# Softmax of the queries for a whole group at once, with a newly searched order

## The chip, the cores and the metric

The kernel runs on one core of one Trainium2 chip. The time is that of one execution on the device, in microseconds (us); the profile is of one further execution on the same core, and its own times run from the first to the last instruction (the span). The engines are TensorE (PE; PEld is its load of weights), VectorE (DVE), ScalarE (ACT), GpSimd (POOL) and SyncE (SP), which here only issues transfers.

## The reference

Two parts follow one another. In the first, q, k and v have 8 batches, 8 heads, 576 positions and 64 features. q is put through a softmax over its 64 features, k through one over the positions; then each head multiplies its k (transposed) with v, and q with that 64x64 result. In the second, the 8 heads side by side make 4608 rows of 512 features, which pass a feed-forward layer.

```python
q_s = np.exp(q - np.max(q, axis=-1, keepdims=True))
q_s = q_s / (np.sum(q_s, axis=-1, keepdims=True) + 1e-09)
k_s = np.exp(k - np.max(k, axis=2, keepdims=True))
k_s = k_s / (np.sum(k_s, axis=2, keepdims=True) + 1e-09)
kv = np.einsum('bhsd,bhse->bhde', k_s, v)
attn = np.einsum('bhsd,bhde->bhse', q_s, kv)
x = attn.transpose(0, 2, 1, 3).reshape(B * S, H * D)
h = x @ w_in                                  # 512 -> 2048
out = (h / (1.0 + np.exp(-1.702 * h))) @ w_out  # 2048 -> 512
```

## The kernel before, in words

The 4608 rows are cut into 12 tiles of 384 (t = 0 to 11), three rows to a partition. A tile's q comes in two groups of four heads (i = 0, 1): 128 partitions with 4 heads x 3 rows x 64 features, 768 values each, in the buffer qt[i]. There are thus 24 groups of q, each with 12 softmaxes to a partition.

`q_stats` makes the softmax of one group. VectorE takes the 12 maxima, with the sign turned, into stat (run_m, L659). ScalarE then executes 12 exponentials of 64 values, each with its own maximum as bias and with a sum taken on the way (run_e, L667: an ACTIVATE and a read of the accumulator each); for the planner these are three or four separate pieces. VectorE adds 1e-9 and takes reciprocals (run_r, L675 and L676). In tiles 0 and 1 VectorE scales the group (run_n, L684) and TensorE transposes it (q_tr, L737). In later tiles (TURNED = 2) a copy of q that is stored turned in DRAM comes in as qT; `spread_out` transposes the statistics (L695), writes them to DRAM (dm and ds, L702), and GpSimd's transfers bring them back spread over partitions (L718): the maxima are added to qT by the transfer itself, then ScalarE takes the exponential of qT (L725, 128x768); the reciprocals overwrite qt, and x_raw (L753) multiplies the product with them.

`k_max` and `k_sub` do the softmax of k (maxima over positions through GpSimd; L552 to L558, L576, L581). `kv_pairs` (L614) multiplies k and v, `x_pairs` (L803) multiplies q with the result.

All matrix products of the feed-forward layer are made from two rounded parts of each operand, a high and a low one, in three matmuls (high-high, high-low, low-high). So every value passes a rounding cast on ScalarE and a subtraction on VectorE (L1265 and L1268, L840 and L843, L1137 and L1140) before TensorE can use it. Weights come in 64-bit form and are converted first (`conv_w`: L439, L443, L447, L454, L464), then stored to DRAM and read back when needed (`refill`, L903). Tiles 0 and 1 run plainly (`g1`, L831; `g2`, L863). From tile 2 on, tiles go in pairs through seven products (`product`, L1230) in place of eight, from sums and differences of the blocks of x (`t_make`, L1083; `x_split`) and of the weights: `s_make` (L1026 to L1041) makes and stores those of w_in, `w_make` (L974 to L1004) those of w_out, once, while tiles 2 and 3 run, from w_out blocks that are refilled for it. For tiles 2 and 3 the second matrix runs plainly (L1494), from tile 4 on in seven products too (`stream` and `still_part`, both through L1366). Results leave through copies (L876, L1456, L1467, L1515) and transfers.

The order of all work is written out by hand. `Plan.add` collects 3333 pieces with engine, cost, buffers read and written, and a function that issues them; the list FIRST gives each piece its place. `Plan.order` walks through the pieces in the sense of this list and issues them, so every engine's queue, and SP's and GpSimd's queues of transfers too, have the order that the list says. A queue executes strictly one after the other: an instruction that waits for a semaphore keeps back all that stand behind it. The costs of `add` serve this walk alone. Rank and table arguments have no further effect on the order once FIRST is given, but ScalarE must load another function table wherever an exponential follows a gelu in its queue, or the other way round.

Of the kernel before, what the change touches and what calls it, by code (L numbers as in the profile page):

```python
# [17 lines left out]
class Plan:  # L18
# [278 lines left out]
def act(n):  # L297
    return 0.19 + n / 1200
# [3 lines left out]
def efficient_attention_then_gelu_ffn(  # L302
# [177 lines left out]
    def bc(a, n):  # L480
        return a.unsqueeze(len(a.shape)).broadcast_to([*a.shape, n])
# [1342 lines left out]
```

## Time and profile before

| | |
|---|---|
| median of 3 runs | 870.77 us (869.83 to 873.27) |
| the profiled execution | 870.66 us |
| its span | 868.9 us, 15873 instructions |
| TensorE busy | 808.8 us (93%) |
| VectorE busy | 564.8 us (65%) |
| ScalarE busy | 581.7 us (67%) |
| GpSimd busy | 166.7 us (19%) |
| mean granted TensorE clock | 0.98 of full speed |
| moved by DMA | 253.72 MB, mean 292 GB/s |
| chain that ended last | TensorE 54%, DMA 21%, VectorE 6%, ScalarE 5% |

A busy time is the union of an engine's instructions, so it counts overlapped ones once. Idle time of an engine matters only if work that the end depends on stands behind it. The names out<-in are the program's tiles: qt, qT and stat are the buffers of the softmax, bank is a PSUM bank, w any weight slot, dwo, dwi, dsl and the like are the copies of weights in DRAM, xc and pu are rounded parts, sl is the scratch of w_make, work and g are temporaries.

### The profile page before, as it was taken

The numbers are of one execution on the slowest core, as the hardware profiler recorded it, in microseconds if no ns is written. First come the engines' busy times: TensorE is split into PE (matmuls) and PEld (weight loads), VectorE is DVE, ScalarE is ACT, GpSimd is POOL, SyncE is SP. The second block draws the span as 40 slices with busy tenths as digits, with TensorE's granted clock in tenths as the row PEclk, the third lists the DMA queues.
The fourth block names the chain that finished last, engine by engine and source line by source line (L and its number), as shares of the span: only waits on it lengthen the run. The fifth ranks groups of instructions, "written<-read, shape, count | busy, mean of one in ns | idle before, by whom it ended". The sixth has DMA issues, their size and how long they took to land.

```text
span 868.9 us, 15873 instructions
## 1 busy us (share of the span) xinstructions
PE 808.8 (93%) x5596; PEld 747.6 (86%) x5596; DVE 564.8 (65%) x1073; ACT 581.7 (67%) x1437; POOL 166.7 (19%) x261
## 2 busy tenths in 40 slices
PE   4799999988899989998999999999999999999998
PEld 3588888767787777787999998999998999999998
DVE  6898953397666577464587755778555497554464
ACT  7988865777675678575687476698576764454443
POOL 1104210534231210232123022222022200000000
PEclk7899999998999999999999999999999999999999
DMA  8998996757999997999988979999789787786861
GB/s 315 409 409 356 330 412 233 186 191 228 372 284 375 297 325 220 343 336 336 319 282 269 322 253 380 297 334 273 240 305 289 251 287 274 234 288 229 300 240 55
DMA packets 98239, 253.72 MB, mean 292 GB/s; under 512 B 14960, under 2 KB 42224, under 8 KB 98160
## 3 DMA queue, kind: packets, MB, share of 16 engines
q1 hardware_dynamic: 86000, 236.72, 75.8%
q0 software_dynamic: 12160, 15.99, 9.5%
q8 instruction: 44, 0.72, 0.3%
q14 instruction: 35, 0.29, 0.1%
HBM read 205.23 MB, written 47.43 MB: 291 GB/s over the span
## 4 chain that ended last, share of the span: by engine, by line
PE 54%; DMA 21%; DVE 6%; ACT 5%; issue 2%; POOL 1%; SPq 1%; DVEq 0%; POOLq 0%; ACTq 0%
PE bank L1230 23%; PE bank L1366 20%; PE bank L1494 4%; DMA qt<-in_q 4%; DMA out<-tmp 3%; DMA qT<-dm 2%; PE bank L831 2%; ACT qt L667 2%; DMA w<-dwo 2%; PE bank L863 2%; DMA w<-dsl 1%; DMA qt<-ds 1%; PE bank L614 1%; DMA w<-dsh 1%; PE bank L803 1%
## 5 line engine op out<-in xcount | busy, mean ns | idle before, releaser
L1230 PE MATMUL bank<-xc,w 128*128 128x384 f32 x1680 | 321.7, 341 | 23.3 <-ACT g L1272 4.8
L1230 PEld LDWEIGHTS bank<-xc,w 128*128 128x128 f32 x1680 | 291.4, 189 | 37.0 <-ACT g L1272 7.6
L1366 PE MATMUL bank<-w,pu 128*128 128x256 f32 x1260 | 163.7, 281 | 1.7 <-DMA w<-dwo 1.2
L1366 PEld LDWEIGHTS bank<-w,pu 128*128 128x128 f32 x1260 | 156.7, 189 | 4.8 <-issue 2.6
L1366 PE MATMUL bank<-w,xc 128*128 128x256 f32 x756 | 102.4, 282 | 4.7 <-DMA w<-dwo 3.3
L1366 PEld LDWEIGHTS bank<-w,xc 128*128 128x128 f32 x756 | 97.0, 189 | 7.7 <-DMA w<-dwo 3.4
L667 ACT ACTIVATE qt<-qt,stat 128x64 f32<-128x64 f32 x288 | 96.4, 337 | 10.2 <-DVE stat L659 7.5
L702 POOL DMA_DIRECT2D dm<-statT x80 | 42.3, 538 | 242.9 <-DVE statT L695 242.6
L831 PE MATMUL bank<-xh,w 128*128 128x384 f32 x256 | 69.5, 341 | 1.3 <-ACT g L837 1.2
L863 PE MATMUL bank<-w,gh 128*128 128x512 f32 x192 | 60.3, 395 | 0.0
L702 POOL DMA_DIRECT2D ds<-statT x80 | 42.8, 607 | 75.1 <-DVE statT L695 74.8
L667 ACT ACTIVATION_READ_ACCUMULATOR qt<-qt,stat 128x1 f32 x288 | 54.4, 189 | 0.0
L718 POOL DMA_DIRECT2D qT<-dm x40 | 38.0, 1075 | 74.0 <-PE bank L1230 37.5
L831 PEld LDWEIGHTS bank<-xh,w 128*128 128x128 f32 x256 | 47.2, 190 | 3.0 <-ACT g L837 2.0
L1272 ACT COPY g<-bank 128x384 f32<-128x384 f32 x52 | 24.8, 477 | 28.3 <-PE bank L1230 22.9
L1272 ACT COPY bank<-bank 128x384 f32<-128x384 f32 x40 | 18.6, 466 | 37.4 <-PE bank L1230 33.4
L831 PE MATMUL bank<-xl,w 128*128 128x384 f32 x128 | 43.3, 338 | 0.0
L863 PEld LDWEIGHTS bank<-w,gh 128*128 128x128 f32 x192 | 35.4, 188 | 8.4 <-issue 1.8
L718 POOL DMA_DIRECT2D qt<-ds x40 | 25.7, 646 | 74.9 <-DMA ds<-statT 20.2
L863 PE MATMUL bank<-w,gl 128*128 128x512 f32 x96 | 38.1, 396 | 1.4 <-DVE gl L843 1.4
L659 DVE TENSOR_REDUCE stat<-qt 128x12 f32<-128x768 f32 x24 | 22.8, 951 | 25.1 <-DMA qt<-in_q 24.9
L1257 ACT ACTIVATE g<-bank 128x384 f32<-128x384 f32 x51 | 25.0, 490 | 21.0 <-PE bank L1230 19.3
(179 smaller groups left out, 1350.0 us busy)
## 6 DMA issues: line engine op xcount, KB each, us to landing
w<-dwo SPq DMA_DIRECT2D x48, 512.0 KB, 5.9
w<-dwb SPq DMA_DIRECT2D x48, 512.0 KB, 5.9
w<-dwi SPq DMA_DIRECT2D x44, 512.0 KB, 6.9
w<-dsl SPq DMA_DIRECT2D x32, 512.0 KB, 6.2
w<-dsh SPq DMA_DIRECT2D x32, 512.0 KB, 6.0
w<-dwa SPq DMA_DIRECT2D x32, 512.0 KB, 6.1
qt<-in_q SPq DMA_DIRECT2D x24, 384.0 KB, 4.8
vt<-in_v SPq DMA_DIRECT2D x14, 650.0 KB, 10.3
```

The source lines that it names most:

```text
L614: nc.tensor.matmul(pk[r0 : r0 + D, m // 2, m % 2], kt[:, o + a, c, :], vt[:, o + a, c, :], start=c == 0, stop=c == CM - 1, tile_position=( ...
L659: nc.vector.tensor_reduce(out=least, in_=qt, axis=AX.X, op=ALU.max, negate=True)
L667: nc.scalar.activation(qt[:, a, b], qt[:, a, b], AF.Exp, bias=least[:, a, b : b + 1], accum_out=sums[:, a, b : b + 1])
L702: nc.gpsimd.dma_start(out=d[:, 32 * b : 32 * b + 32], in_=statT[i][at_ : at_ + M, :])
L718: nc.gpsimd.dma_start(out=out_, in_=src, **more)
L831: nc.tensor.matmul(ph, wi[w][j][:, c, :], x[:, c, :], start=c == 0 and i == 0, stop=c == KC - 1 and i == 2,)
L863: nc.tensor.matmul(po[c], x[:, cs], wo[w][j], start=j == 0 and i == 0, stop=j == NJ - 1 and i == 2)
L1230: nc.tensor.matmul(pb, ws[w][:, c * P : (c + 1) * P], xx[x][:, c * TB : (c + 1) * TB], start=p in FRESH and c == 0 and i == 0, stop=c == 1 ...
L1257: lambda: nc.scalar.activation(d, src, AF.Gelu_apprx_sigmoid), table="gelu")
L1272: plan.add("ACT", act(TB), (PB,), (key,), free_, lambda: nc.scalar.copy(dst, pb))
L1366: nc.tensor.matmul(po, y[:, cs], w, start=start and i == 0, stop=i == 2, skip_group_check=True,)
L1494: nc.tensor.matmul(po[:, f0:f1], x[:, cs], w[:, h * DM + f0 : h * DM + f1], start=m == 0 and e == 0 and i == 0, stop=m == NQ - 1 and e == ...
```

## The change

In `q_stats` the per-head exponentials are taken out of ScalarE's list. VectorE adds the (negative) maxima to the whole group, with the 12 maxima broadcast over 64 features; ScalarE takes one exponential over the group in place; VectorE sums the 12 runs of 64 into stat. The gate, which holds the work back to a stage, moves from the exponentials to the addition. For a group of tiles 2 and up this makes three pieces out of four, for one of tiles 0 and 1 three out of three, so there are 3313 pieces, and FIRST is a new list throughout.

```diff
@@ FIRST: all 3333 places replaced by 3313 others @@
-    1328, 1, 2, 12, 10, 11, 13, 15, 4, 0, 3, 5, 7, 6, 8, 37, 44, 39, 70, 42, 64, 61, 58, 67, 76, 86, 142, 128, 146,
...
@@ in q_stats @@
-        def run_e(a):
-            for b in range(qt.shape[2]):
-                nc.scalar.activation(
-                    qt[:, a, b], qt[:, a, b], AF.Exp, bias=least[:, a, b : b + 1], accum_out=sums[:, a, b : b + 1]
-                )
-
-        for a in range(qt.shape[1]):
-            plan.add("ACT", 0.25 * qt.shape[2], (KM, *gate), (*Q, KS), ranks[1], lambda a=a: run_e(a), table="exp")
+        def run_s():
+            nc.vector.tensor_tensor(out=qt, in0=qt, in1=bc(least, D), op=ALU.add)
+
+        plan.add("DVE", dve(M * D), (KM, *gate), Q, ranks[1], run_s)
+        plan.add("ACT", act(M * D), (), Q, ranks[1], lambda: nc.scalar.activation(qt, qt, AF.Exp), table="exp")
+
+        def run_t():
+            nc.vector.tensor_reduce(out=sums, in_=qt, axis=AX.X, op=ALU.add)
+
+        plan.add("DVE", dve(M * D), Q, (KS,), ranks[2], run_t)
```

How the two lists differ, piece by piece: of TensorE's 730 pieces 443 have another place in its queue, 100 by more than three places and none by more than 16. Of VectorE's pieces that both kernels have, 376 of 1036 move by more than three places, of ScalarE's 169 of 827 (a group's exponentials counted as one), of SP's transfers 174 of 535, of GpSimd's 15 of 137. In the first transfers, the second batch's two k loads are issued before v's instead of behind the weights w_in 0 and w_out 0.

## Rows read from the trace of the kernel before

**Rows 1.** The page: busy us and share by engine; TensorE's costliest group with mean ns.

```profile
PE 808.8 (93%) x5596; PEld 747.6 (86%) x5596; DVE 564.8 (65%) x1073; ACT 581.7 (67%) x1437; POOL 166.7 (19%) x261
...
L1230 PE MATMUL bank<-xc,w 128*128 128x384 f32 x1680 | 321.7, 341 | 23.3 <-ACT g L1272 4.8
```

**Rows 2.** Stretches: us, busy by engine, clock, DMA share, GB/s.

```profile
0.00:34.00 34.00, 18.47 (x175) 13.96 (x176) 24.30 (x48) 26.63 (x102) 5.82 (x9) 0.78 0.91 349
34.00:145.00 111.00, 108.31 (x608) 96.85 (x608) 80.94 (x120) 84.47 (x171) 19.34 (x27) 0.99 0.95 361
145.00:215.00 70.00, 60.76 (x420) 49.99 (x420) 45.57 (x90) 49.74 (x152) 30.57 (x48) 0.93 0.69 202
215.00:375.00 160.00, 146.77 (x809) 125.41 (x808) 107.33 (x220) 111.27 (x284) 34.75 (x57) 0.98 0.94 317
375.00:700.00 325.00, 310.91 (x2385) 298.54 (x2384) 209.06 (x414) 229.12 (x563) 76.17 (x122) 1.00 0.91 298
```

**Rows 3.** TensorE's waits: releaser, us in total, times, longest.

```profile
PE bank L737 <- ACT qt L667: 4.9, 1, 4.9
...
PE bank L1366 <- DMA w<-dwo: 4.5, 2, 3.3
...
PE bank L1230 <- DMA w<-dsl: 2.2, 2, 1.3
```

**Rows 4.** Timeline, TensorE and one of VectorE: start, us, what, [idle before <-releaser].

```profile
158.21 2.55 PE L614 MATMUL bank<-vt,kt 128*64 128x65 f32 x80 [1.27 <-ACT tmp L876]
...
191.10 0.44 PE L1230 MATMUL bank<-xc,w 128*128 128x384 f32 x1 [0.97 <-ACT xc L1137]
...
230.83 0.95 DVE L659 TENSOR_REDUCE stat<-qt 128x12 f32<-128x768 f32 x1 [4.50 <-DMA qt<-in_q]
...
233.88 1.56 PE L803 MATMUL bank<-qT,kvn 64*64 64x192 f32 x16 [3.37 <-issue]
...
263.67 1.64 PE L1230 MATMUL bank<-xc,w 128*128 128x384 f32 x6 [1.96 <-DVE g L1249]
...
306.59 1.31 PE L1230 MATMUL bank<-xc,w 128*128 128x384 f32 x6 [2.94 <-DVE raw L753]
```

**Rows 5.** Groups by line and form: busy us, mean ns, idle before by releaser.

```profile
L659 DVE TENSOR_REDUCE stat<-qt 128x12 f32<-128x768 f32 x24 | 22.8, 951 | 25.1 <-DMA qt<-in_q 24.9
...
L684 DVE TENSOR_TENSOR qt<-qt,stat 128x768 f32<-128x768 f32 x4 | 3.8, 958 | 0.1
...
L725 ACT ACTIVATE qT<-qT 128x768 f32<-128x768 f32 x20 | 16.9, 845 | 4.1 <-DMA qT<-dm 3.2 <-issue 0.8
```

**Rows 6.** VectorE's waits: the first sums of w_make.

```profile
DVE sl L974 <- DMA w<-dwo: 15.8, 11, 4.4
```

**Rows 7.** Groups by line and form, line 667.

```profile
L667 ACT ACTIVATE qt<-qt,stat 128x64 f32<-128x64 f32 x288 | 96.4, 337 | 10.2 <-DVE stat L659 7.5 <-DVE statT L695 2.5
...
L667 ACT ACT_TABLE_LOAD x15 | 19.2, 1283 | 0.7 <-DMA qt<-in_q 0.4
```

**Rows 8.** Line 667 over six stretches of the span: its busy time summed.

```profile
sum 868.90, ACT 120.61; mean ACT 20.10
```

**Rows 9.** Timeline of ScalarE: a table load and the activation behind it.

```profile
182.32 1.28 ACT L725 ACT_TABLE_LOAD   x1
183.61 0.84 ACT L725 ACTIVATE qT<-qT 128x768 f32<-128x768 f32 x1
```

**Rows 10.** Timeline of the start: VectorE, then the first large matmul.

```profile
7.78 0.69 DVE L552 TENSOR_TENSOR tmp<-kt 128x512 f32<-128x512 f32 x1 [2.58 <-DMA kt<-in_k]
...
28.54 1.48 DVE L576 TENSOR_TENSOR ek<-ek,mx 128x1280 f32<-128x1280 f32 x1
...
33.74 0.69 PE L831 MATMUL bank<-xh,w 128*128 128x384 f32 x1
```

**Rows 11.** The page, DMA issues: KB each, median us to landing.

```profile
w<-dwo SPq DMA_DIRECT2D x48, 512.0 KB, 5.9
...
qt<-in_q SPq DMA_DIRECT2D x24, 384.0 KB, 4.8
```

346 rows, old and new, of the table FIRST are left out of this document.

## The prediction, made before the changed kernel was run

> **What bounds the kernel now.** I read the page's busy times first, then a table by stretches, then whom TensorE waited for, then its single idle gaps, each with the queue of the engine that it names. TensorE is busy 808.8 of 868.9 us [rows 1]. The missing 60.1 us is all that a change to VectorE and ScalarE can win, apart from the slow clock in two stretches. The table puts 15.5 us of it into the first 34 us (18.47 busy, granted clock 0.78), 2.7 into the next 111, 9.2 into the turn from 145 to 215 (clock 0.93), 13.2 into 215 to 375 and 14.1 into 375 to 700 [rows 2]; some 5 us lie behind that, where no q is left. No helper is full: ScalarE is busy 67% and VectorE 65%. Both are dense at the start (26.63 and 24.30 of 34).
>
> TensorE's largest single wait is the first transpose of q, 4.9 us; 6.7 us were spent waiting for weights from DRAM, on two rows [rows 3]. The gaps one by one show another cause: at 263.67 and 306.59 TensorE waits 1.96 and 2.94 us for VectorE, and at 233.88 it waits 3.37 us with no releaser named [rows 4]. VectorE itself then stands at the head of its queue waiting for a transfer: the maximum of a q group at 230.83 had waited 4.50 us for the load of q, with other work behind it [rows 4]. Over the run such maxima wait 24.9 us [rows 5], and the first sums of w_make (L974) 15.8 us for w_out blocks [rows 6]. So this is a TensorE-bound kernel whose remaining gaps come from the start, from dense ScalarE and VectorE at the turn, and from transfers that land after the place that the written order gave their reader.
>
> **What is removed and added, in engine time.** Per group of q, 12 activations with a bias and a sum each go. Line 667 holds ScalarE for 120.61 us; without its 15 table loads of 1.283 (19.2) that is 101.4, or 4.22 for each of 24 groups [rows 7, 8]. One exponential of 128x768 takes their place; the same form stands in the trace as L725, 0.845 us. Saved: 24 x (4.22 - 0.85) = 81 us. VectorE gets an addition of 128x768 with a broadcast operand (the form of L684, 0.958) and a sum of 128x768 to 128x12 (the form of the maximum, L659, 0.951) [rows 5]: 24 x 1.91 = 46 us more. From the end of the maximum to the sums it takes 2.8 us instead of 4.2 if nothing stands between.
>
> The searched order also sets how often ScalarE changes its function table: counted in the written order, 58 times before (as many loads as the trace has, 15 of them at L667 [rows 7]) and 64 after; 6 x 1.283 = 7.7 us. ScalarE thus ends near 582 - 81 + 8 = 509 us busy, VectorE near 565 + 46 = 611: the fuller helper is now VectorE.
>
> The trace shows what a switch takes in the queue: a load begins at 182.32, and the activation behind it at 183.61 [rows 9], 1.29 us later. The Trainium skill (ScalarE: Activation LUTs, What ACT_TABLE_LOAD costs) says that about 1.38 us of draining follow each load, 2.66 per switch; by that the six switches would cost 16 us of ScalarE instead of 7.7. The row disagrees, and I go by the row.
>
> **The start (to about 60 us).** Four of the groups lie here. ScalarE gains 4 x 3.37 = 13.5 us, VectorE gets 4 x 1.91 = 7.6 more. On VectorE, the work that leads to the first large matmul (33.74) passes the subtraction for the second batch's k at 28.54 [rows 10]. In the new list five of the new instructions stand ahead of it (4.8 us). The third group's scaling (0.96) and two conversion steps of 128x512 (0.69 each at most, what such a step takes at 7.78) are moved behind it, 2.3. The first addition falls into the 2.58 us in which VectorE waits for k at 7.78 [rows 10], 0.96 covered. Net 4.8 - 2.3 - 1.0 = 1.5 us later; of VectorE's 9.7 us idle in the first 34 [rows 2] some, between 9 and 28 us, can give a part back. The third group's sum and scaling now stand ahead of the transpose that TensorE executes before the second batch's key-value product, and the fourth group's follow among conversions, while TensorE idles only 2.7 of the next 111 us. I take +1.5 in all. The 4.9 us wait for the first transpose hardly shrinks: the first sum stands in VectorE's new list behind three steps for k's maximum, which begin at 7.78, and the next q's maximum; what ScalarE gains is lost there. Bounds: -3 (the loads of the second batch's k are issued ahead of v, and ScalarE stops being a limit, a quarter of its 13.5) to +6.7 (7.6 less the covered 0.96).
>
> **The turn (145 to 215).** Two gaps follow directly on a run of line 667: 1.27 us at 158.21, where a copy of an output bank (L876) stood behind 24 of its activations, and 0.97 at 191.10, where the split of x (L1137) stood behind nine [rows 4]. In the new list the second group's exponential of the third tile stands later, behind such casts. I take both, -2.2. Bounds: 0 to -6, two thirds of the stretch's 9.2 us idle.
>
> **Late transfers.** I counted the steps of TensorE's written order that stand between the issue of a load and its first reader; a step is a product or its like, six matmuls, 6 x 321.7 / 1680 = 1.15 us [rows 1]. Of the 16 refills that w_make reads, 11 had four steps or fewer before, none has after; the median goes from 4 to 9.5. Of the 24 loads of q, those with three or fewer fall from 8 to 5, the median goes from 4 to 5. Of 268 refills that TensorE reads itself, those with four or fewer fall from 11 to 5, and none is left with three. A w_out block lands 5.9 us after its issue, q 4.8 [rows 11]: four steps are too few for the one and about even for the other, nine are enough. So the two gaps behind w_make go (1.96 + 2.94 = 4.9), half of the 3.37 at 233.88 (its load of q has 8 steps instead of 6), and a quarter of the 6.7 us of direct waits, 1.7: together -8.3. Bounds: -15.0 (all of these whole) to +3, one gap of the largest size newly made, since a load issued earlier needs its buffer earlier, and all loads stand in SP's queue behind the one that waits.
>
> **New waits elsewhere.** 20 groups put 38 us on VectorE between 60 and 700 us. Maximum, addition and sum stand in one queue with the splits (L1268) and sums (L1249) that TensorE needs, and the sum waits there for ScalarE's exponential; whatever is behind it is late by that wait. Where the new list leaves a few steps between exponential and sum, as it mostly does, the wait is nothing; I take +1.5, bounds 0 to +5 (a quarter us per group). Of the six table loads I take one on the path, +1.3, bounds 0 to +7.7.
>
> **Sum.** +1.5 - 2.2 - 8.3 + 1.5 + 1.3 = -6.2. The profiled execution took 870.66 us (its span of 868.9 and 1.8 around it), 0.1 below the median of 870.77: 870.77 - 6.2 = 864.6.
>
> **Rivals.**
> - The gaps change places. TensorE executes the same matmuls in nearly the same order (100 of 730 steps move by more than three), and where one wait goes, the next bank may wait for its copy instead. For it: each gap is only 1 to 3 us. Against it: the late transfers are one cause, which the order takes away. Gains of 10.5 shrink to a third, the costs of 4.3 stay: 870.8 - 3.5 + 4.3 = 871.6.
> - Slower: VectorE becomes the limit of the start. Place: its queue from 12 to 60 us, where the conversion of weights waits behind the new instructions. Price: +6.7, with the costs elsewhere (+2.8) against a third of the transfer gain (-2.8): 877.5. It decides when the subtraction for the second batch's k begins after about 31 us and the first large matmul after 37. Against it: conversions of weights needed later can slip at no cost.
> - A large gain: all late-transfer gaps go (-15.0) and the turn gives 3, at the costs of 4.3: 857.1. For it: the shortest distances grow for all kinds of loads. Against it: five refills keep four steps.
>
> **Chances.** Forecast 0.50, places change 0.22, large gain 0.13, slower 0.15. A measurement of this kernel tells about 0.5% from no change, 4.4 us: faster is below 866.4, slower above 875.1. The forecast's own range, 859 to 869, gives 0.46 faster and 0.04 same; the large gain 0.13 faster; the changed places 0.03, 0.16 and 0.03; the slow start 0.01 same and 0.14 slower. Faster 0.62, same 0.21, slower 0.17. The range is 853 to 877: it leaves out about half of the slow case and the ends of the large gain.
>
> **What would show it.** Right: ScalarE near 509 and VectorE near 611 us busy; 64 table loads; VectorE's wait of L974 for w_out down from 15.8 to under 5, and of the maxima for q under 18; no gap of TensorE over 2.5 us between 215 and 375; the first large matmul between 33 and 36.5 us. Wrong: 10 us or more of new gaps in front of VectorE's splits, a first large matmul after 37, or more than 6.7 us of direct waits of TensorE for w_out and low slab refills.

## The result, and the profile after

Before and after were run on one chip: 872.02 us median before (869.83 to 873.81, 4 runs), 840.33 after (838.14 to 845.29, 4 runs). The ratio is 0.9646, with a 95% interval of 0.9595 to 0.9696. The forecast of 864.6 had the direction right and a fifth of the size; the time lies 13 us below the range. The profiled execution of the changed kernel took 840.9 us, its span 839.1. In the table below, ratios leave out runs more than 1.5% above the fastest of their kernel and medians do not, so for f3_old_on_time (870.5 to 888.6 us) the median looks worse than the ratio.

The page first; in the changed kernel most lines behind the softmax stand one number higher.

```profile
PE 800.3 (95%) x5596; PEld 744.8 (89%) x5596; DVE 606.9 (72%) x1121; ACT 515.6 (61%) x891; POOL 166.7 (20%) x261
...
L1231 PE MATMUL bank<-xc,w 128*128 128x384 f32 x1680 | 318.7, 337 | 13.7 <-DVE g L1250 4.2
```

Against [rows 1], TensorE's idle time fell from 60.1 to 38.8 us (839.1 - 800.3), 21.3 of the 29.8 us of span. The other 8.5 us came out of its busy time, with the same 5596 matmuls. VectorE and ScalarE moved as forecast (611 and 509 expected).

The page's groups of the new softmax (line, engine, operation, out<-in, count, busy us, mean ns, idle before):

```profile
L665 DVE TENSOR_TENSOR qt<-qt,stat 128x768 f32<-128x768 f32 x24 | 22.7, 950 | 0.1
...
L668 ACT ACTIVATE qt<-qt 128x768 f32<-128x768 f32 x24 | 20.3, 846 | 6.4 <-DVE qt L665 6.3
...
L671 DVE TENSOR_REDUCE stat<-qt 128x12 f32<-128x768 f32 x24 | 22.7, 947 | 0.9 <-ACT qt L668 0.6
```

The durations taken from the nearest forms [rows 5] were right within 10 ns. The stretches of [rows 2], in the kernel after:

```profile
0.00:34.00 34.00, 18.30 (x177) 14.91 (x178) 28.46 (x53) 16.66 (x28) 4.18 (x8) 0.75 0.95 375
34.00:145.00 111.00, 109.88 (x620) 97.13 (x619) 85.89 (x129) 73.03 (x104) 19.97 (x27) 1.00 0.93 347
145.00:215.00 70.00, 64.50 (x451) 53.84 (x451) 55.18 (x103) 45.87 (x70) 31.30 (x48) 0.95 0.85 253
215.00:375.00 160.00, 155.91 (x963) 136.40 (x962) 127.31 (x248) 107.03 (x183) 41.85 (x66) 1.00 1.00 331
375.00:700.00 325.00, 315.79 (x2404) 306.99 (x2403) 234.96 (x448) 210.60 (x375) 69.40 (x112) 1.00 0.92 306
```

Between 215 and 375 us TensorE executed 963 instructions where it had executed 809. But equal times no longer hold equal work, so I cut both spans where TensorE had done about the same number of instructions (the marks agree within 15). The kernel before:

```profile
0.00:33.74 33.74, 18.21 (x174) 13.70 (x174) 24.07 (x47) 26.37 (x101) 5.56 (x9) 0.78 0.91 348
33.74:152.90 119.16, 116.47 (x648) 103.06 (x647) 86.27 (x130) 90.38 (x198) 22.16 (x32) 0.99 0.93 351
152.90:185.60 32.70, 28.89 (x215) 23.55 (x214) 18.33 (x37) 20.53 (x51) 14.63 (x22) 1.00 0.68 195
185.60:402.20 216.60, 193.28 (x1195) 167.09 (x1195) 143.88 (x292) 150.02 (x396) 57.17 (x92) 0.96 0.92 308
402.20:868.90 466.70, 451.92 (x3370) 440.20 (x3368) 292.26 (x571) 294.42 (x698) 67.12 (x109) 1.00 0.82 272
```

The kernel after:

```profile
0.00:33.45 33.45, 17.75 (x174) 14.36 (x175) 27.94 (x51) 16.28 (x27) 4.18 (x8) 0.74 0.95 374
33.45:147.10 113.65, 112.53 (x633) 99.40 (x632) 87.78 (x134) 74.32 (x106) 19.97 (x27) 1.00 0.93 343
147.10:181.60 34.50, 32.85 (x225) 26.51 (x224) 26.59 (x48) 18.53 (x27) 17.91 (x26) 0.95 0.78 230
181.60:378.00 196.40, 188.45 (x1202) 165.01 (x1201) 156.05 (x302) 134.53 (x228) 55.24 (x88) 0.99 0.99 324
378.00:839.10 461.10, 448.74 (x3370) 439.57 (x3369) 308.57 (x590) 271.99 (x506) 69.40 (x112) 1.00 0.85 283
```

The fourth row is the one to read: tiles 2 and 3, in which w_make makes its sums while TensorE runs products, took 20.2 us less (216.60 to 196.40). 15.4 of that is idle time (23.3 to 7.95), 4.8 is busy time at a higher clock (0.96 to 0.99). The start is equal; 5.5 us went between 34 and 150 (about half of it because the stretch after holds 15 instructions fewer, at 0.18 us each), 5.6 behind tile 3, and the third stretch became 1.8 longer.

TensorE's waits, as in [rows 3] (releaser, us in total, times, longest):

```profile
PE bank L613 <- ACT kt L580: 4.9, 2, 3.4
PE bank L1231 <- DVE g L1250: 4.2, 3, 1.8
PE bank L738 <- DVE qt L685: 3.9, 3, 2.1
PE bank L1367 <- DMA w<-dwo: 2.9, 2, 2.7
PE bank L1231 <- DMA w<-dwi: 2.8, 2, 1.7
PE bank L1231 <- ACT bank L1273: 2.3, 3, 1.0
```

And VectorE's waits for transfers, as the first row of [rows 5] and [rows 6]:

```profile
DVE stat L658 <- DMA qt<-in_q: 17.3, 9, 4.8
...
DVE sl L975 <- DMA dwb<-sl: 5.9, 4, 2.6
```

The sums of w_make no longer wait for w_out blocks at all (15.8 us before); they wait 5.9 us for a store of their own scratch (sl) instead, 1.1 before. The sum over all rows of TensorE's waits by engine, without the one for the identity matrix at the start, is a surprise: waits put down to transfers fell only from 8.7 to 5.7 us, those put down to ScalarE from 25.1 to 12.7, to VectorE from 15.0 to 10.9, and the 3.4 us without a releaser are gone. Nor do the transfers land earlier: a w_out block takes 6.5 us from issue to landing and q 6.3, where [rows 11] have 5.9 and 4.8.

### The profile page after: what moved, and what is told of

Its sections match the earlier page's. It is cut to its first block, busy times and chain, and to the rows that moved or that the text cites. A ratio compares the mean times of both kernels' runs of the same rounds, so it can differ in the third digit from the quotient of the medians.

```text
span 839.1 us, 15303 instructions
## 1 busy us (share of the span) xinstructions
PE 800.3 (95%) x5596; PEld 744.8 (89%) x5596; DVE 606.9 (72%) x1121; ACT 515.6 (61%) x891; POOL 166.7 (20%) x261
## 4 chain that ended last, share of the span: by engine, by line
PE 70%; DMA 16%; DVE 8%; issue 2%; ACT 2%; SPq 1%; POOL 0%; DVEq 0%; ACTq 0%; POOLq 0%
PE bank L1231 27%; PE bank L1367 24%; PE bank L864 6%; PE bank L832 6%; PE bank L1495 6%; DMA w<-dwo 3%; DMA qt<-in_q 3%; DMA ds<-statT 2%; DMA qT<-dm 2%; DMA w<-dwi 2%; PE bank L804 1%; DMA w<-dwa 1%; DMA qt<-ds 1%; DMA dwb<-xc 1%; DMA dwb<-sl 1%
## 5 line engine op out<-in xcount | busy, mean ns | idle before, releaser
L838 ACT ACTIVATE g<-bank 128x384 f32<-128x384 f32 x32 | 15.6, 490 | 37.4 <-PE bank L832 32.9
L1250 DVE TENSOR_TENSOR g<-bank,g 128x384 f32<-128x384 f32 x33 | 18.3, 554 | 28.0 <-PE bank L1231 27.5
L1269 DVE TENSOR_TENSOR pu<-g,pu 128x384 fp32r<-128x384 f32 x47 | 26.4, 564 | 16.6 <-ACT pu L1266 16.2
L1258 ACT ACTIVATE g<-bank 128x384 f32<-128x384 f32 x51 | 25.1, 492 | 21.5 <-PE bank L1231 16.3
```

The costliest lines, as they stand in the source:

```text
L838: nc.scalar.activation(gt, ph, AF.Gelu_apprx_sigmoid)
L1250: lambda: nc.vector.tensor_tensor(out=d, in0=pb, in1=o, op=ALU.add),
L1258: lambda: nc.scalar.activation(d, src, AF.Gelu_apprx_sigmoid), table="gelu")
L1269: lambda: nc.vector.tensor_tensor(out=get()[1], in0=d, in1=get()[0].bitcast(F32), op=ALU.subtract),
```

## The experiments

Three theories stood at the outset. (A) The list gains by giving readers more room behind their transfers. (B) The softmax gains, by relieving ScalarE. (C) Softmax and list are worth something only together. Ratios are to the kernel before, run on the same chip in turn, with 95% intervals. "Idle" and "busy" are TensorE's in the profiled run; before has 60.1 and 808.8, after 38.8 and 800.3.

| kernel | softmax | list | median us | ratio [interval] | idle | busy |
|---|---|---|---|---|---|---|
| c_old_order | new | before's | 875.4 | 1.005 [1.001, 1.008] | 61.1 | 811.0 |
| d_old_softmax | old | after's | 883.8 | 1.013 [1.008, 1.019] | 67.7 | 814.7 |
| e1_w_make_later | old | before's, edited | 888.8 | 1.019 [1.012, 1.027] | 76.0 | 811.4 |
| e2_max_later | old | before's, edited | 893.7 | 1.024 [1.017, 1.031] | 78.5 | 815.5 |
| f3_old_on_time | old | searched, on time | 882.7 | 1.005 [0.999, 1.011] | 64.5 | 810.0 |
| h2_old_on_time2 | old | searched, on time | 871.9 | 0.999 [0.996, 1.003] | 62.2 | 811.8 |
| h1_new_on_time | new | searched, on time | 874.7 | 1.000 [0.995, 1.004] | 59.0 | 811.5 |
| f1_old_searched | old | searched, late | 847.1 | 0.967 [0.962, 0.973] | 45.3 | 799.5 |
| g3_old_second | old | searched, late | 853.1 | 0.981 [0.977, 0.985] | 49.6 | 803.8 |
| h3_old_third | old | searched, late | 846.4 | 0.967 [0.962, 0.972] | 41.1 | 802.0 |
| f2_new_searched | new | searched, late | 844.0 | 0.963 [0.958, 0.968] | 40.6 | 800.1 |
| g4_new_second | new | searched, late | 833.1 | 0.959 [0.955, 0.964] | 32.5 | 798.5 |
| h4_new_third | new | searched, late | 834.3 | 0.953 [0.947, 0.959] | 38.9 | 795.3 |
| f4_after_searched | new | after's, searched on, late | 839.7 | 0.958 [0.952, 0.965] | 40.3 | 802.2 |
| g1_sp_late | old | searched, SyncE's late | 859.9 | 0.987 [0.982, 0.991] | 52.4 | 803.8 |
| g2_pool_late | old | searched, GpSimd's late | 863.6 | 0.991 [0.987, 0.995] | 51.4 | 803.6 |
| i1_before_half | old | before's, half refills | 844.8 | 0.968 [0.965, 0.972] | 40.1 | 801.4 |
| i2_third_half | old | h3's, half refills | 835.1 | 0.956 [0.954, 0.959] | 33.2 | 800.4 |

**The two parts alone.** c_old_order is the changed kernel with before's list (a group's addition and exponential in the place of its first exponentials, the sum ahead of the reciprocals). d_old_softmax is the changed kernel with its list, and the 12 activations as one piece in the place of the one exponential.

```diff
@@ c_old_order: FIRST of after.py @@
-    531, 2, 1, 34, 12, 16, 18, 20, 4, 0, 3, 8,
+    1319, 1, 2, 12, 10, 11, 13, 16, 4, 0, 3, 5,
...
@@ d_old_softmax: q_stats of after.py @@
-            nc.vector.tensor_tensor(out=qt, in0=qt, in1=bc(least, D), op=ALU.add)
...
-        plan.add("ACT", act(M * D), (), Q, ranks[1], lambda: nc.scalar.activation(qt, qt, AF.Exp), table="exp")
...
+                    nc.scalar.activation(
+                        qt[:, a, b], qt[:, a, b], AF.Exp, bias=least[:, a, b : b + 1], accum_out=sums[:, a, b : b + 1]
+                    )
```

> The new softmax in the old order: every piece keeps its old place; the addition stands directly ahead of where a group's first exponential stood, the one exponential there, the sum directly ahead of the reciprocal. Theory 'order' (the gain of 31 us comes from readers that the new list puts further behind their transfers): little of it is here, 862 to 874 us, VectorE's waits of L974 for w_out stay near 15 us and of the maxima for q above 20. Theory 'ScalarE' (the gain comes from 66 us less work on ScalarE): 840 to 852 us.

> The old softmax in the new order: the 12 activations with their sums stand where the new list has the one exponential, addition and sum are empty. Theory 'order': 840 to 852 us, waits for transfers as in the changed kernel. Theory 'ScalarE': 860 to 872 us, with ScalarE back near 585 us busy.

Over the whole run neither part keeps any of the gain: c is 0.5% slower than before, d 1.3%. Both also lie above every range that was set down for them. In c TensorE waits at the start for the scaled q, and VectorE's late transfers are nearly what they were [rows 5, 6]:

```profile
PE bank L732 <- DVE qt L679: 10.7, 3, 7.0
...
DVE stat L652 <- DMA qt<-in_q: 23.8, 12, 4.1
DVE sl L969 <- DMA w<-dwo: 13.1, 9, 4.2
```

So relieving ScalarE of about 75 us (581.7 to 507.1 busy in c) buys nothing by itself: theory B falls. In d the waits of w_make for w_out are gone as in the changed kernel, but TensorE waits 9.2 us for ScalarE's copies of banks where before it waited 2.6 for them: a block of 12 activations (4.2 us) takes the place of one of 0.85 ahead of such copies; before had it in three or four pieces, so d is somewhat coarser than the old softmax. That a list fits only the pieces for which it was searched may be read from this, but is not shown, as the pieces are coarser too.

```profile
PE bank L1231 <- ACT bank L1273: 9.2, 6, 2.7
```

The total hides that d does gain in one place. Cut where TensorE had executed about as many instructions as at 185.6 and 402.2 us in before, it is 10.0 us faster in tiles 2 and 3 (216.60 before) and 16.8 slower behind them (466.70 before):

```profile
192.30:398.90 206.60, 190.85 (x1196) 168.21 (x1195) 142.94 (x289) 155.54 (x390) 56.19 (x90) 0.97 0.94 309
398.90:882.40 483.50, 457.51 (x3365) 446.20 (x3364) 293.29 (x568) 299.49 (x710) 68.57 (x111) 0.98 0.81 269
```

**Readers moved by hand.** Theory A in its simplest form: take before, and let only the late readers stand later. In e1_w_make_later seven of the eight blocks of w_make, all but their transfers, go 4 of TensorE's steps down; in e2_max_later 16 maxima of q go down until 8 steps lie between load and maximum. What needs them is pushed behind; all else keeps its order.

```diff
@@ e1_w_make_later: FIRST of before.py, as the text says @@
-    1328, 1, 2, 12, 10, 11, 13, 15, 4, 0, 3, 5,
+    1315, 1, 2, 12, 10, 11, 13, 15, 4, 0, 3, 5,
...
@@ e2_max_later: FIRST of before.py, as the text says; from within @@
-    585, 587, 619, 685, 693, 695, 799, 746,
+    585, 587, 619, 695, 697, 698, 799, 746,
...
```

> The kernel before with one part of the new order: seven of the eight w_make (all but the first) have their sums and casts four TensorE steps later in the list, with what depends on them. Theory 'order', in the form of the prediction (w_make's late refills alone cost two gaps of TensorE, 4.9 us): 862 to 868 us, VectorE's wait of L974 for w_out from 15.8 to under 4. Theory 'ScalarE': no change, 868 to 875.

> The kernel before with another part: 16 maxima of q from tile 3 on that stood up to six TensorE steps behind their load stand eight behind it, with what depends on them. Theory 'order': 863 to 869 us, VectorE's wait for q from 24.9 to under 8 us. Theory 'ScalarE': no change or slower, 868 to 878, since the exponentials come later on a full ScalarE.

The waits went, as wanted: in e1 that of [rows 6] fell from 15.8 to 7.0 us, in e2 that of the maxima from 24.9 [rows 5] to 7.9; in e1 the sums wait 11.0 us for a store of their scratch instead (1.1 before). The time rose by 17 and 22 us. The waits of VectorE, of ScalarE and of TensorE in e1:

```profile
DVE sl L968 <- DMA w<-dwo: 7.0, 3, 3.3
...
DVE sl L968 <- DMA dwb<-sl: 11.0, 3, 6.6
```

```profile
ACT xc L974 <- DVE sl L971: 22.8, 6, 8.1
```

```profile
PE bank L1224 <- ACT g L1266: 11.2, 6, 6.0
PE bank L1224 <- ACT work L1251: 7.1, 1, 7.1
```

ScalarE's rounding of the sums waited 22.8 us for VectorE (7.8 before), up to 8.1 at once, and TensorE up to 7.1 us at once for ScalarE. The wait was not taken away; it changed its name and grew. A reader can't be moved alone: what stands behind it in its queue, and the buffers that it frees, move too (which of the two cost the time, no run shows). Theory A falls in this form.

**Lists searched anew.** A program of mine moves pieces within their engines' queues at random and keeps what ends earlier when the list is walked with the pieces' costs. "Late" lists were walked with every transfer landing 2.1 us after its last byte and again with 3.5 us, with half the weight each; "on time" lists with 2.1 us alone. Nothing else differs, and the kernels' code is that of before (old softmax) or after (new), with another FIRST.

```diff
@@ f1_old_searched, f3_old_on_time: FIRST of before.py @@
-    1328, 1, 2, 12, 10, 11, 13, 15, 4, 0, 3, 5,
+    83, 1, 3, 8, 35, 39, 42, 47, 2, 0, 5, 10,
+    39, 4, 2, 45, 18, 21, 24, 29, 3, 0, 5, 6,
...
@@ f2_new_searched, f4_after_searched: FIRST of after.py @@
-    531, 2, 1, 34, 12, 16, 18, 20, 4, 0, 3, 8,
+    2255, 5, 1, 27, 26, 31, 53, 56, 2, 0, 6, 8,
+    458, 4, 2, 27, 33, 37, 41, 44, 1, 0, 3, 10,
...
```

> The old softmax with a list that I searched from the old one: single pieces are moved within their engine's queue, and a move is kept by the planner's own walk, with its table loads and transfers, once with transfers that land 2.1 us after their last byte (the planner's value) and once 3.5 us; an exponential piece has the duration that the trace shows. Theory 'search' (a list searched anew for late transfers gives most of the 31 us with either softmax): 835 to 850 us. Theory 'pair' (the new softmax is needed, the old one cannot go far below 860 with any list): 855 to 872 us.

> The new softmax with a list searched in the same way and for as long, from the old list as in c_old_order. Both theories: 830 to 848 us. Its distance to f1_old_searched is what the softmax is worth when each has its own list: under 'search' 0 to 8 us, under 'pair' 15 or more.

> As f1_old_searched, but the search takes only transfers that land on the planner's 2.1 us. Theory 'late' (what counts is the room behind transfers): 8 us or more slower than f1_old_searched, VectorE's and TensorE's waits for transfers clearly longer. Otherwise (what counts is the list as a whole): within 5 us of f1_old_searched.

> The new softmax with a list searched in the same way from the changed kernel's own list. If that list can still be bettered: 828 to 838 us; if the walk has nothing more to say about the chip: 838 to 845.

f1 gains 3.3% without the new softmax; f3, the same search with transfers on time, gains nothing. f4 shows that the changed kernel's own list, searched on, gives no clear gain over it (839.7 against 840.3 us, intervals overlapping). The pages of f1 and f3:

```profile
PE 799.5 (95%) x5596; PEld 743.1 (88%) x5596; DVE 559.2 (66%) x1073; ACT 594.2 (70%) x1449; POOL 165.9 (20%) x261
```

```profile
PE 810.0 (93%) x5596; PEld 752.5 (86%) x5596; DVE 562.5 (64%) x1073; ACT 598.5 (68%) x1453; POOL 163.2 (19%) x261
```

ScalarE is as full in the one as in the other; what differs is TensorE's idle time (45.3 against 64.5) and its busy time (799.5 against 810.0). One mark of f3 did not come: waits for transfers were to be clearly longer in it. Without the first wait of the run, TensorE's rows with the name of a transfer sum to 8.6 us in f3 and 4.6 in f1, VectorE's to 41.1 and 37.0; it is the rows with ScalarE's name that part them, 27.1 against 5.5.

Nor is f3 slow everywhere. In tiles 2 and 3 and behind them, cut in the same way as d, f3 and then f1:

```profile
186.00:390.10 204.10, 188.16 (x1198) 164.49 (x1197) 143.90 (x290) 154.02 (x382) 53.98 (x87) 0.98 0.96 324
390.10:874.50 484.40, 457.34 (x3365) 445.60 (x3363) 289.41 (x571) 301.40 (x718) 70.24 (x114) 0.99 0.79 270
...
187.70:386.20 198.50, 185.63 (x1198) 162.99 (x1197) 141.72 (x287) 151.40 (x371) 55.46 (x88) 0.99 1.00 333
386.20:844.80 458.60, 450.96 (x3365) 439.73 (x3363) 290.84 (x573) 298.96 (x715) 70.27 (x112) 1.00 0.85 284
```

f3 took 12.5 us less than before in tiles 2 and 3 and 17.7 us more behind them; f1 took 18.1 and 8.1 us less.

**Which transfers, and two more pairs.** g1 and g2 let only SyncE's or only GpSimd's transfers be late in the search; g3 and g4 repeat f1 and f2 from another random start, h3 and h4 from a third; h1 fills the empty cell (new softmax, on time), h2 repeats f3.

```diff
@@ g1, g2, g3, h2, h3: FIRST of before.py @@
-    1328, 1, 2, 12, 10, 11, 13, 15, 4, 0, 3, 5,
+    2390, 1, 4, 8, 30, 34, 38, 42, 3, 0, 2, 37,
+    1990, 5, 3, 33, 21, 25, 43, 55, 6, 1, 0, 12,
+    2260, 1, 3, 8, 34, 62, 71, 74, 2, 0, 6, 14,
+    995, 6, 1, 58, 28, 38, 41, 46, 4, 0, 2, 11,
+    2257, 3, 1, 38, 14, 17, 31, 36, 5, 0, 2, 11,
...
@@ g4, h1, h4: FIRST of after.py @@
-    531, 2, 1, 34, 12, 16, 18, 20, 4, 0, 3, 8,
+    970, 6, 2, 72, 27, 29, 36, 55, 1, 0, 3, 11,
+    1724, 2, 1, 13, 12, 39, 52, 57, 4, 3, 0, 16,
+    2159, 6, 2, 36, 29, 32, 60, 70, 5, 1, 0, 11,
...
```

> The softmax of before, with a list searched with only SyncE's loads and refills landing late (2.1 and 3.5 us after the last byte) and GpSimd's transfers always at 2.1. If the gain of such a search comes from room behind SyncE's transfers (w_out, w_in and x refills, the loads of q), 845 to 855 us, as with both late (847.1). If the room behind GpSimd's spreads and selections is what counts, 866 to 882. Both count: 855 to 866.

> The softmax of before, with a list searched with only GpSimd's transfers landing late and SyncE's always at 2.1 us. Theory of SyncE's transfers: 868 to 882 us, near the list searched with everything on time (882.7 beside a before of about 878, ratio 1.005). Theory of GpSimd's spreads: 845 to 855. Both count: 855 to 866.

> The softmax of before, a second search with both kinds of transfers late from another random start. If room behind transfers is what the list is worth, and not luck of one list, 842 to 853 us; if the first list (847.1) was luck, anything from 855 to 880.

> The softmax of the change, a second search with both kinds of transfers late from another random start. 838 to 850 us if the list carries the gain. Against the second list of the old softmax: the softmax alone is worth 3 us (the first pair, 847.1 and 844.0) if the pairs agree; the rival, that the softmax is worth most of the gain once the list suits it, wants 10 us or more between them.

> The softmax of the change, with a list searched with every transfer at 2.1 us. If the gain needs both the softmax and late transfers in the search, 862 to 880 us, near the old softmax so searched (ratio 1.005). If the softmax is worth something whatever the search, 845 to 862, that is 10 us or more below its partners f3 and h2.

> The softmax of before, a second search with every transfer at 2.1 us. If a search on time gives nothing on the chip, 866 to 885 us; if f3 was an unlucky list, 848 to 862.

> The softmax of before, a third search with both kinds of transfers late. 845 to 855 us from the first two (847.1 and 853.1).

> The softmax of the change, a third search with both kinds of transfers late. 832 to 845 us from the first two (844.0 and 833.1). The softmax is worth 3 us if this comes within 5 us of the old softmax's third list, some 10 if 8 to 15 below, 20 if more.

Three lists searched on time lie at 0.999 to 1.005 with either softmax; six searched late (without f4, which started from another list) lie at 0.953 to 0.981. The other two on time do as f3 does: cut in the same way, h1 and h2 gain 12.3 and 10.0 us in tiles 2 and 3 and lose 14.4 and 11.9 behind. With the old softmax the late search is worth 2.8% on average (0.967, 0.981, 0.967), some 25 us. Each kind of transfer alone gave about a third to a half of it (0.987 and 0.991), with one list each. The new softmax adds 3.1, 20.0 and 12.2 us in the three pairs of late lists (847.1 - 844.0, 853.1 - 833.1, 846.4 - 834.3) and nothing between lists searched on time. So theory C holds for a part of the gain, the smaller one in two pairs and half of it in the second (20.0 of 39.2 us); the rest needs the list alone. Lists of one kind differ among themselves by up to 11 us, so the pairs give its sign and not its size. g4 and h4 are also the fastest kernels found: 833.1 and 834.3 us, where after has 840.3 (ratios 0.959 and 0.953 against 0.965; g4's interval overlaps that of after, h4's ends just below it).

**Lateness itself.** The lists show that a search under late transfers pays, not yet that lateness is what costs the old list its time on the chip. i1 and i2 make the 236 refills of 512 KB land earlier, in the same way in before and in h3: they read only the first half of each block, and the other half of the buffer keeps what it held, so their results are not the kernel's.

```diff
@@ refill: i1 in before.py, i2 in h3_old_third.py @@
                 to, of = (x.rearrange("p (s f) -> p s f", s=2)[:, :, part] for x in (to, of))
+            else:
+                to, of = to[:, :DM], of[:, :DM]
             nc.sync.dma_start(out=to, in_=of)
```

> The kernel before, in which the 236 refills of 512 KB read only the first half of their block (256 KB); the other half of each buffer keeps what it held, so results are left wrong in part, and 60 of 254 MB are not moved. If late landings are what its list loses its time to: 845 to 862 us, a gain of 10 to 25. If the list loses its time to something else (waits among engines that no transfer causes): 866 to 874.

> The same halving in the old softmax's third list searched under late transfers (846.4 whole). If late landings are the cause and this list stands them already: 838 to 847, a gain of at most 8, less than half of what the kernel before gains. If both kernels gain alike, the halving helps in a way that has nothing to do with the list.

The issues of two transfers in i1 (KB each, median us to landing), where [rows 11] have 5.9 and 4.8:

```profile
w<-dwo SPq DMA_DIRECT2D x48, 256.0 KB, 3.9
...
qt<-in_q SPq DMA_DIRECT2D x24, 384.0 KB, 4.5
```

Before gained 30 us (0.968 [0.965, 0.972]) with no other edit, as much as the whole change or a late list brings; h3, which has such a list, gained 11 (846.4 to 835.1; the two ran on different chips, where before took 873.9 and 874.8). Both gained more than was expected of lateness as the cause (10 to 25 and at most 8). The mark that tells was that h3 gains less than half as much, and it does: the late list had already taken nearly two thirds of what earlier landing gives the old one (30 - 11 of 30). The halving is broad: with some 60 MB less to move GpSimd's 192 KB spreads land earlier too (qT<-dm 5.6 us where before has 7.1). It does not work through shorter instructions: VectorE and ScalarE are busy 565.4 and 581.0 us in i1, 564.8 and 581.7 in before. The remaining distance between the two lists is 10 us (844.8 against 835.1), where it was 27; those 10 are not the halved refills. A rival is that any relief brings less to a better list. The one other relief on record speaks against it, since the new softmax brought nothing on before's list and 3 to 20 us on late ones. No run halves the refills of the changed kernel itself, so that its list gains in the same way as h3's is an inference. In i1 the gain lies where the change has it, in tiles 2 and 3. First the row over the very times that held 1195 instructions and 193.28 us of work in before, then the one from mark to mark (216.60 us in before, so 18.0 of the 27.4 us that the span lost):

```profile
185.60:402.20 216.60, 205.05 (x1309) 180.86 (x1308) 155.01 (x315) 159.98 (x421) 62.20 (x100) 0.98 0.85 266
...
185.20:383.80 198.60, 188.63 (x1197) 165.47 (x1196) 144.31 (x290) 149.39 (x397) 57.49 (x92) 0.97 0.84 267
```

And of the waits that I had taken for the whole matter, VectorE's:

```profile
DVE stat L659 <- DMA qt<-in_q: 15.8, 11, 3.0
...
DVE sl L976 <- DMA w<-dwo: 3.4, 3, 2.6
```

Where the 27.4 us had stood in TensorE's rows can be read off too. Waits with the name of a transfer fell from 8.7 us to nothing, ScalarE's from 25.1 to 22.1, VectorE's from 15.0 to 9.8, those without a releaser from 3.4 to 0.5, and busy time from 808.8 to 801.4.

## Why the prediction was wrong

**Engine time: right.** ScalarE 515.6 against 509, VectorE 606.9 against 611, 64 table loads, the three forms within 10 ns. That this leaves no gain by itself was right as well: the prediction gave the softmax no credit beyond the turn, and c shows 0.5% loss.

**The start (+1.5): right in kind.** c has the softmax's price there: its first 200 TensorE instructions end 3.3 us later than before's, inside the bounds. In the changed kernel the first large matmul begins at 33.45 (33.74 before); the list took the price back. The wait for the first transpose did shrink, against the prediction, from 4.9 to 2.1 us, while the key-value products now wait 4.9 for k's exponential. What was won behind the start, up to 150 us, I had not seen: the stretch had only 2.7 us idle [rows 2].

**The turn (-2.2): right in its gaps, wrong in time.** Both gaps that were to go are gone. Idle time between the equal marks fell from 3.81 to 1.65 us, by just 2.2, but that is luck: the second gap (191.10) lies behind the mark, and another, of 0.94 us, went in its place. And the clock there was 0.95 instead of 1.00, and the stretch became 1.8 us longer, 10 of its 225 matmuls being additional.

**Late transfers (-8.3): the step that failed.** The two stretches with q or w_make behind the turn became 25.8 us shorter (20.2 + 5.6), 17.8 of it idle time. That late transfers are the place to look was right, as far as i1 and the late lists show; the size was not, and its outer bound of -15.0 fell with it. The step went wrong in three ways.
- It added up gaps that carried the name of a transfer, or stood directly behind a reader that had waited for one. i1 shows what earlier landing of the refills is worth to the same list: 30 us, 27.4 of span in the profiled runs, of which the rows with a transfer's name held 8.7. Another 8.2 had stood as waits for ScalarE and VectorE, 2.9 without a releaser and 7.4 as busy time. In the changed kernel the names moved otherwise: 3.0 us from the rows of transfers, 12.4 from ScalarE's, 4.1 from VectorE's. A VectorE queue that stands 4.5 us at its head [rows 4] makes late all that is behind it, and TensorE can meet that delay further on, under the name of the engine it then waits for; that this is the way of those us is argued, not followed through the trace.
- It measured room as steps between issue and first reader. (Its 268 refills that TensorE reads are 248; the other 20 are read by w_make and s_make. The counts of short ones stand.) f3 shows that the measure does not price a list: counted in the same way, its list has a median of 11.5 steps in front of w_make (after 9.5, before 4), 5 loads of q with three or fewer (after 5, before 8), and 4 refills with four or fewer (after 5, before 11). By the prediction's rule f3 had to gain like the change. In tiles 2 and 3 it did gain 12.5 us of the change's 20.2, but it lost 17.7 behind them, where the rule saw nothing wrong. e1 and e2, which have more room and are slower, say the same from the other side.
- It left the clock out ("apart from the slow clock in two stretches"). TensorE's busy time fell by 8.5 us with its idle time.

**New waits (+1.5) and table loads (+1.3): not found.** Sums waited 0.6 us for their exponentials in all (L671). One row of TensorE's waits for VectorE's L1250 rose by 2.0 us (2.2 to 4.2), but all rows with that line together fell from 6.7 to 4.9. The 64 table loads came as counted; whether one lies on the path, no run tells.

**What was to show it.** Every mark of being right came true: ScalarE and VectorE within 7 us, 64 table loads, no wait of w_make for w_out, maxima 17.3 us (under 18), the largest gap of TensorE between 215 and 375 us 1.57 (under 2.5), the first large matmul at 33.45 (33 to 36.5). The forecast could be right by all of its marks and still 24 us off, as they looked at the named waits again. The rival "a large gain" named the cause that the runs point to, and took its size from the same list of gaps.

**What stays open.** Which property of a list makes it stand late transfers isn't named by any run: the count of steps is not enough. Lists searched late and on time part most behind tile 3 (25.8 of the 29.7 us between f1 and f3), while the changed kernel gained most in tiles 2 and 3; why on-time lists lose behind tile 3 was not followed up. GpSimd's transfers, which the prediction didn't count at all, gave a third of the gain in the one list whose search had them alone late. How much of the change is due to its softmax can't be told apart either: its 0.965 [0.960, 0.970] overlaps the best that the old softmax reaches (0.967), and the pairs give 3 to 20 us.

## What to carry to other kernels

In a kernel whose order is fixed, price late transfers by making them land earlier in the chip run (half the bytes, all else equal) before adding up the waits that bear their name: here the names held 8.7 of the 27 us that the span lost. An order that is searched should be searched with transfers that land later than the planner's value too; searched on time, it gave nothing in three attempts, searched late, it gained 2 to 5% in six. Moving single readers back by hand, each of them the cause of a plain gap, made the kernel slower both times. And compare lists stretch by stretch, cut at equal counts of instructions: the totals of d and f3 hide that each gained 10 us or more in tiles 2 and 3.

## What the runs showed of the hardware

TensorE's busy time for the same 5596 matmuls rises with its idle time: 795.3 us where it idled 38.9 (h4), 808.8 where it idled 60.1 (before), 815.5 where it idled 78.5 (e2). Between these ends that is half a microsecond more of busy time for each microsecond idle (20.2 over 39.6), with scatter: g4 idled 32.5 and was busy 798.5, and a line through all 20 runs gives 0.4. Not each stretch follows it, as the turn shows.

The granted clock accounts for it. Its mean over the span is 0.980 before, 0.995 in h4 and 0.969 in e2, and busy time multiplied by it gives 793, 791 and 790 us; over all 20 runs the product lies between 787 and 797. The mean is a mixture of two levels. In before the stretch from 193 to 203 us was granted 0.50, the lower of them (1.2 of 2.4 GHz), after TensorE had waited 0.97 and 0.55 us in the 3 us ahead of it:

```profile
193.00:203.00 10.00, 8.27 (x44) 6.82 (x44) 7.00 (x14) 8.62 (x34) 4.58 (x9) 0.50 0.48 112
```
